# Narrowing MoE2's weights as a pipeline over three pieces, and splitting the token combinations at the MoEs' border from the tiles that form them

## The chip, the cores and the metric

One Trainium2 chip, one of its cores. The metric is the device time of one launch in microseconds (us), lower is better. Three runs of the kernel before gave 1250.58, 1254.18 and 1259.58 us; the median is 1254.18 us.

## The reference, cut to what matters

Attention with talking heads feeds two MoE layers (one expert each) one after the other. Everything is float32 in the reference; the inputs of the MoEs' weights are float64 on the host and reach the chip as 64-bit words.

```python
# attention: batch 4, 12 heads, 448 positions, head_dim 64
scores = softmax(einsum('bhij,hg->bgij', scale * q @ k.T, w_pre))
x = einsum('bhij,hg->bgij', scores, w_post) @ v        # -> [1792 tokens, 768]
# MoE1: w_in 768x1024, w_out 1024x768
h = x @ w_in
solu = h * softmax(h)
x = ((solu - mean) / sqrt(var + 1e-6) * g_ln) @ w_out
# MoE2: w_in 768x2048, w_out 2048x768
g = maximum(x @ w_in, 0) ** 2
out = g @ w_out
```

## The kernel before

The kernel is one program whose order is written by hand: every engine runs its instructions in the order of the code, and a tile's buffers (`bufs=`) decide when an instruction may start. TensorE (PE) multiplies; ScalarE (ACT), VectorE (DVE) and GpSimd (POOL) do the rest; SyncE's queue (SP) issues nearly all DMAs, in order. Float32 products are made of three products of high and low parts, so each operand is split: ACT writes the high part, and DVE or POOL subtracts it to get the low part.

**Stages.** Attention runs to about 406 us. MoE1 follows: a loop over 14 tiles of 128 tokens (m = 0 to 13, line 828). The border between the MoEs finishes MoE1's output products and prepares MoE2 (`prepare`, line 990). MoE2 (line 1170) runs 16 steps q: eight slices of 256 hidden columns for the first half of the tokens, then the same eight for the second half. Its input product is a Strassen-like scheme with seven products p1 to p7 (`prod`) over halves of tokens and of channels, which needs sums and differences of token blocks (`mix_x`) and of weight blocks (`mix_w`).

**A tile of MoE1.** PE does `h1(m)` (36 matmuls), transposes tile m-1 (`zt`, 8) and, from m = 4 on, two output products (`out1`, 24 each). `norm1(m)` takes the negative maximum (DVE, line 712), the exponential (ACT, 715), the gated product and its statistics (DVE, 718 to 723), a power (POOL, 725 and 726), and, behind a yield, the normalisation (ACT, 732). The transposes of the next tile wait for that. In tiles 0 to 3, two blocks of MoE1's output weights are loaded per tile (`load_w1_out`, 683) and split at once by ACT (688) and POOL (689).

**Narrowing.** MoE2's weights arrive as 96 pieces of 128x256 64-bit words. `w2stream` turns each into float32 bits and stores it in HBM, from where MoE2 loads slices. It is a generator: the MoE loops call `steps2(n)` to issue its next n steps between their own instructions. A piece is: ACT squares the high words into `sq` (80), DVE makes the bits in three instructions (83, 87, 91), and values whose square is under 2^-30 are made zero. In MoE1 POOL does that (`flush`, a compare at 100 and a product at 101), in MoE2's first half DVE does (96). `nraw` has three buffers, `nt` two, `nsq` one. 65 pieces are narrowed in MoE1 and 31 in MoE2.

**The border.** `mix_x(0)` loads blocks `xb` of MoE1's output x2D, forms four combinations on DVE and stores them in HBM (`xtD`). `load_xc` then loads each operand again into `xr` (three buffers), and `split_xc` splits it (ACT 925, DVE 926). p1, p6, p5 and p7 are split during the last nine output products, p3, p2 and p4 in the first three slots of step q = 0. For the second half of the tokens POOL does `mix_x` during q = 2 to 6.

Of the kernel before, what the change touches and what calls it, by code (L numbers as in the profile page):

```python
# [18 lines left out]
def kernel(  # L19
# [761 lines left out]
    def w2stream():  # L781

        raws, ready = {}, []

# [12 lines left out]
        load(0)
        load(1)
        for i in range(len(w2pieces)):
            sq = nar_p.tile([128, WP], F32, tag="nsq", name="nsq", bufs=1)  # L800
            t = nar_p.tile([128, WP], F32, tag="nt", name="nt", bufs=2)
            eng = nc.gpsimd if in_first else nc.vector
            for step, _ in enumerate(narrow(raws[i], sq, t, eng)):
                if step == 1:
                    load(i + 2)
                if step == 2 and ready:
                    store()
                yield True
            if eng is nc.gpsimd:
                flush(sq, t)  # L810
# [62 lines left out]
    def mix_x(p, eng):  # L873
# [2 lines left out]
        parts = {}
        for c in range(HC + 1):
            if c < HC:
                qs = []
                for k in range(2):  # L880
                    for t in range(2):
# [383 lines left out]
```

## Time and profile before

| what | value |
|---|---|
| median of three runs | 1254.18 us |
| the profiled execution's own time | 1259.37 us |
| its span, first to last instruction | 1257.6 us |
| mean granted TensorE clock | 0.940 |
| busy share PE, DVE, POOL, ACT | 86%, 59%, 56%, 47% |
| PE busy, 409.7 to 795.7 us | 287.6 of 386.0 us |
| PE busy, 970.7 us to the end | 280.0 of 286.9 us |

A row of the timeline gives the start, the length, the engine, the line and what is written from what; brackets hold the engine's idle time before it and what ended that. A row of a tile's answer gives the shortest, median and longest duration in ns. A row that names an instruction and two numbers below "idle" or "waited" gives microseconds and times.

### The profile page before, as it was taken

The page shows a single profiled execution, that of the slowest core. Times are in us where ns is not written, and L with a number is a line of the kernel's source. Part 1 is how long each engine was busy: PE and PEld are TensorE (multiplying, and loading weights), DVE is VectorE, ACT ScalarE, POOL GpSimd, SP SyncE. Part 2 cuts the span into 40 slices and gives each one's busy share as a digit, 9 for nine tenths or more (in the row PEclk, how much of TensorE's full clock was granted, in tenths as well). Part 3 has the DMA queues.
Part 4 walks back from the last instruction along what each step waited for, and adds up shares of the span by engine and source line. Part 5 has one row for each costly group of instructions (what it writes and reads, how often), then busy time and mean ns, then how long its engine had stood idle before and what let it go on. Part 6 is the DMA issues. An engine that isn't in the chain of part 4 may idle for free.

```text
span 1257.6 us, 31153 instructions
## 1 busy us (share of the span) xinstructions
PE 1083.1 (86%) x12488; PEld 908.4 (72%) x12488; DVE 738.3 (59%) x1293; ACT 585.0 (47%) x1212; POOL 699.9 (56%) x910
## 2 busy tenths in 40 slices
PE   8898979889898855898798666998889999999998
PEld 3555656556667644687687666888778899999998
DVE  3557768658662644555556455778877563344444
ACT  4666666668663322332332224643434556444432
POOL 3657988877755554453554353556654655555531
PEclk9899999989998977898999787999989999999999
DMA  6777887777664433343343485454443352222102
GB/s 178 207 219 221 236 249 219 234 219 209 203 194 121 147 105 112 114 143 97 115 142 107 141 289 163 125 175 142 143 142 106 117 179 99 66 73 63 51 26 88
DMA packets 131936, 187.91 MB, mean 149 GB/s; under 512 B 24752, under 2 KB 104368, under 8 KB 131792
## 3 DMA queue, kind: packets, MB, share of 16 engines
q1 hardware_dynamic: 122948, 161.40, 41.7%
q0 software_dynamic: 6464, 22.60, 6.6%
q10 hardware_dynamic: 2380, 1.93, 0.6%
q8 instruction: 98, 1.61, 0.6%
q14 instruction: 46, 0.38, 0.1%
HBM read 106.45 MB, written 40.89 MB: 117 GB/s over the span
## 4 chain that ended last, share of the span: by engine, by line
PE 20%; DVE 16%; DMA 11%; issue 7%; POOL 6%; ACT 5%; SPq 1%; POOLq 0%; DVEq 0%; ACTq 0%
PE ps_y L1119 11%; PE ps_h L1050 9%; DMA w2iD<-nt 3%; DVE nt L87 2%; POOL nt L101 2%; DMA w2oD<-nt 2%; POOL nsq L100 2%; DMA xr<-x2D 2%; DVE nt L91 2%; DVE y L1130 2%; DMA xr<-xtD 1%; DVE st L721 1%; DVE e L718 1%; DMA w1oraw<-w1oD 1%; DVE nt L83 1%
## 5 line engine op out<-in xcount | busy, mean ns | idle before, releaser
L1119 PE MATMUL ps_y<-to,gt 128*128 128x384 f32 x1332 | 250.9, 342 | 17.5 <-DVE y L1130 17.2
L1119 PEld LDWEIGHTS ps_y<-to,gt 128*128 128x128 f32 x1332 | 238.8, 192 | 24.0 <-DVE y L1130 18.2
L1050 PE MATMUL ps_h<-xc,ti 128*128 128x448 f32 x1008 | 222.4, 373 | 17.1 <-DVE h L1085 10.7
L1050 PEld LDWEIGHTS ps_h<-xc,ti 128*128 128x128 f32 x1008 | 192.0, 192 | 34.9 <-ACT ti L979 11.0
L761 PE MATMUL ps_o<-zt,w1o 128*128 128x384 f32 (+1 forms) x720 | 136.1, 351 | 30.7 <-ACT o L769 27.9
L761 PEld LDWEIGHTS ps_o<-zt,w1o 128*128 128x128 f32 x720 | 130.2, 209 | 35.3 <-ACT o L769 31.7
L299 PEld LDWEIGHTS ps_ring<-w,e 60*64 60x64 f32 (+1 forms) x5760 | 103.3, 138 | 72.1 <-issue 41.1
L318 DVE COPY at<-ps_ring 128x420 f32<-128x420 f32 x156 | 87.8, 610 | 108.5 <-PE ps_ring L299 108.4
L299 PE MATMUL ps_ring<-w,e 60*64 60x60 f32 (+2 forms) x5760 | 112.2, 222 | 31.8 <-issue 23.8
L80 ACT ACTIVATE nsq<-nraw 128x256 f32<-128x256 f32 x96 | 41.7, 434 | 210.0 <-POOL nt L101 145.6
L215 ACT COPY ssrc<-ps_ring 128x896 f32<-128x896 f32 x92 | 82.3, 906 | 107.3 <-PE ps_ring L208 94.0
L459 PE MATMUL ps_h<-w1i,xs 128*128 128x512 f32 x504 | 126.1, 409 | 3.8 <-POOL xs L702 3.4
L1130 DVE TENSOR_TENSOR y<-ps_y,y 128x768 f32<-128x768 f32 x97 | 92.1, 952 | 50.2 <-PE ps_y L1119 50.2
L260 ACT ACTIVATE e<-ps_pre,nm 128x448 f32<-128x448 f32 x180 | 113.1, 639 | 13.7 <-DVE nm L253 10.8
L459 PEld LDWEIGHTS ps_h<-w1i,xs 128*128 128x128 f32 x504 | 97.9, 196 | 27.7 <-POOL xs L702 4.3
L980 POOL TENSOR_TENSOR ti<-s,ti 128x384 fp32r<-128x384 f32 x64 | 69.6, 1099 | 74.1 <-ACT ti L979 72.5
L253 DVE TENSOR_REDUCE nm<-ps_pre 128x1 f32<-128x448 f32 x180 | 103.2, 611 | 12.4 <-PE ps_pre L242 12.4
L208 PE MATMUL ps_ring<-k,q 64*64 64x448 f32 x752 | 100.7, 558 | 5.6 <-ACT ssrc L215 3.7
L242 PE MATMUL ps_pre<-sdst,wpre_bd 64*64 64x448 f32 x720 | 100.5, 570 | 4.4 <-issue 2.7
L1063 DVE TENSOR_TENSOR gt<-h,gt 128x448 fp32r<-128x448 f32 x64 | 48.7, 761 | 92.0 <-ACT gt L1068 90.4
L338 PEld LDWEIGHTS ps_ring<-at,v 128*64 128x64 f32 x1536 | 77.7, 142 | 31.0 <-PE ps_pre L242 12.0
L83 DVE TENSOR_SCALAR nt<-nraw 128x256 uint32<-128x256 uint32 x96 | 39.3, 409 | 94.0 <-DMA w2iD<-nt 53.8
(112 smaller groups left out, 1660.0 us busy)
## 6 DMA issues: line engine op xcount, KB each, us to landing
sdst<-ssrc SPq DMA_DIRECT2D x166, 210.0 KB
nraw<-in_moe_w_in_dram SPq DMA_DIRECT2D x48, 256.0 KB
nraw<-in_moe_w_out_dram SPq DMA_DIRECT2D x48, 256.0 KB
ra<-w2iD SPq DMA_DIRECT2D x32, 384.0 KB
ro<-w2oD SPq DMA_DIRECT2D x32, 384.0 KB
w1raw<-in_moe_w_in_dram POOLq DMA_DIRECT2D x24, 256.0 KB, 6.3
w1raw<-in_moe_w_out_dram POOLq DMA_DIRECT2D x24, 256.0 KB, 5.7
w2iD<-nt SPq DMA_DIRECT2D x48, 128.0 KB
```

The costliest lines, as they stand in the source:

```text
L208: nc.tensor.matmul(out=ps[64 * u:64 * u + 64, e, 0:S], lhsT=qq[c][64 * e:64 * e + 64, p * n + u * half:p * n + u * half + 64], rhs=k[64 * ...
L215: (nc.vector.tensor_copy if dve else nc.scalar.copy)(ssrc[c][:, p:H:HP, :], ps[:, :, 0:S])
L242: nc.tensor.matmul(out=ps[b][64 * u:64 * u + 64, 0:S], lhsT=wpre_bd[64 * r:64 * r + m], rhs=ds[b][64 * r:64 * r + m], start=True, stop=True,)
L253: nc.vector.tensor_reduce(out=nm, in_=pres[s][b][:, 0:S], op=ALU.max, axis=AX.X, negate=True)
L260: nc.scalar.activation(out=e, in_=pres[s][b][:, 0:S], func=AF.Exp, bias=nms.pop((s, b)), scale=1.0, accum_out=sms[s][:, b:b + 1])
L299: nc.tensor.matmul(out=ps[64 * c:64 * c + 64, u, i0:i0 + ng * RH], lhsT=e[64 * u:64 * u + m, o:o + 64], rhs=w[64 * u:64 * u + m, b, g0:g0 ...
L318: nc.vector.tensor_copy(dst[:, 1:3] if u else dst[:, 0:4:3], pv)
L459: nc.tensor.matmul(out=ps[:, u], lhsT=t[:, a, cc], rhs=w1i[cc][:, w, u * 512:(u + 1) * 512], start=(cc == 0 and a == 0 and w == 0), stop=( ...
L761: nc.tensor.matmul(out=ps[:, 0:width], lhsT=w1o[k][:, w, cc * 128:(cc + 1) * 128], rhs=zT[:, a, k, 0:width], start=(k == 0 and i == 0), st ...
L1050: nc.tensor.matmul(out=bank[b][:, 0:HT], lhsT=t[:, w, c], rhs=xc[name][:, a, c], start=(first and c == 0 and i == 0), stop=(c == HC - 1 an ...
L1119: nc.tensor.matmul(out=ps[:, u - u2[0], 0:DM // 2], lhsT=gt[:, a, f, o:o + 128], rhs=w[:, v, f, u * (DM // 2):(u + 1) * (DM // 2)], start= ...
L1130: nc.vector.tensor_tensor(out=yo, in0=po, in1=yo, op=ALU.add)
```

## The change

1. **Narrowing.** The flush goes. In its place ACT squares the high words straight into the result tile, and POOL turns that into a mask of bits in one instruction (compare, times 2 - 2^-23: all bits that the first DVE step may keep, or none). DVE's first instruction ANDs the shifted bits with the mask instead of a constant. The square and the mask of piece i+1 are issued ahead of piece i's DVE work, and the load runs `nr - 1` pieces ahead: five buffers each for `nraw` and `nt` in MoE1, three each in MoE2. A piece is now three steps, with one DVE instruction each.
2. **Its place.** 60 pieces run in MoE1, in groups of 3, 3, 4 and 4 steps per tile (it was 5, 5, 7 and 7 of five-step pieces). 36 run in MoE2, two steps per slot up to slot 9 and one behind it. The second half of `norm1` moves behind the first output product of the tile.
3. **Buffers.** MoE1's loads of x and of output weights use the buffers of the weight preparation; narrowing has no pool of its own any more.
4. **The border.** `prepare` splits p1, p5, p7 and p6 straight from the `xb` tiles as they are formed; only p4's combination goes through HBM.
5. **Second half.** Its combinations are formed with loads further ahead, and its operands are loaded two ahead, every other one into `xb` buffers.

```diff
+    FIRST = 60
-    def w2stream():
+    def w2stream(todo, pool, nr, nt):
...
+        def mask(i):
+            if i in todo:
+                t = ts[i] = pool.tile([128, WP], F32, tag="nt", name="nt", bufs=nt)
+                nc.scalar.activation(out=t, in_=words(i)[1].bitcast(F32), func=AF.Square)
+                nc.gpsimd.tensor_scalar(
+                    out=t, in0=t, scalar1=2.0**-30, scalar2=2.0 - 2.0**-23, op0=ALU.is_ge, op1=ALU.mult
+                )
...
+        for i in range(nr - 1):
+            load(a + i)
+        mask(a)
+        for i in todo:
+            load(i + nr - 1)
+            mask(i + 1)
+            low, high = words(i)
+            bits = ts[i].bitcast(U32)
+            stt = nc.vector.scalar_tensor_tensor
+            stt(out=bits, in0=high, scalar=3, in1=bits, op0=ALU.logical_shift_left, op1=ALU.bitwise_and)
+            yield True
+            if ready:
+                store()
+            stt(out=bits, in0=high, scalar=0xC0000000, in1=bits, op0=ALU.bitwise_and, op1=ALU.bitwise_or)
+            yield True
+            stt(out=bits, in0=low, scalar=29, in1=bits, op0=ALU.logical_shift_right, op1=ALU.bitwise_or)
...
+    stream = w2stream(range(FIRST), m1b_p, 5, 5)
...
-        steps2(5)
+        steps2(3)
         if m > 0:
             zt(m - 1)
-        run(norm)
-        steps2(5)
+        steps2(3)
...
-        for _ in range(2):
+        for i in range(2):
             if outs:
                 out1(*outs.pop(0))
-            steps2(7 if m else 0)
+            steps2(4 if m else 2)
+            if i == 0:
+                run(norm)
+    run(stream)
...
     def prepare():
         load_ra(0)
-        load_xc(0, "p1")
-        mx = mix_x(0, nc.vector)
...
+        parts = [load_xb(0, 0), load_xb(0, 1)]
...
+        for c in range(HC):
+            b11, b12, b21, b22 = qs = parts[c]
+            split_xc(0, "p1", c, b11)
+            yield True
+            mix_x(qs, 0, nc.vector)
+            mix_x(qs, 1, nc.vector)
+            split_xc(0, "p5", c, b11)
+            yield True
+            mix_x(qs, 2, nc.vector)
+            mix_x(qs, 3, nc.vector)
+            split_xc(0, "p7", c, b12)
+            yield True
+            split_xc(0, "p6", c, b22)
+            store_xt(0, c, "p4", b21)
+            if c + 2 < HC:
+                parts.append(load_xb(0, c + 2))
+            split_ti(0, weights.pop(0))
...
     load_xc(0, ORDER[4])
+    load_ra(1)
...
+    in_second = w2stream(range(FIRST, len(w2pieces)), wi2_p, 3, 3)
+    stream = in_second
...
-                steps2(2 if q else 1)
+                steps2(2 if q and k < 10 else 1)
```

What this moves is shown at three places. First, POOL in tile 1 of MoE1: `w1o` are the two blocks of output weights that it splits, `xs` the tokens of tile 3, `nsq`, `nt` the narrowing. Before:

```order
L100 TENSOR_SCALAR nsq<-nsq 128x256
L101 TENSOR_TENSOR nt<-nt,nsq 128x256
L702 TENSOR_TENSOR xs<-xraw,xs 128x768
L689 TENSOR_TENSOR w1o_7718<-w1oraw,w1o_7718 128x768
L689 TENSOR_TENSOR w1o_7721<-w1oraw,w1o_7721 128x768
L100 TENSOR_SCALAR nsq<-nsq 128x256
L101 TENSOR_TENSOR nt<-nt,nsq 128x256
L100 TENSOR_SCALAR nsq<-nsq 128x256
L101 TENSOR_TENSOR nt<-nt,nsq 128x256
```

The same place now, from the end of the tile's statistics on:

```order
L725 TENSOR_TENSOR rs<-rs,eps_sb 128x1
L800 TENSOR_SCALAR nt<-nt 128x256 x2
L701 TENSOR_TENSOR xs<-xraw,xs 128x768
L687 TENSOR_TENSOR w1o_7726<-w1oraw,w1o_7726 128x768
L687 TENSOR_TENSOR w1o_7729<-w1oraw,w1o_7729 128x768
L800 TENSOR_SCALAR nt<-nt 128x256 x2
```

A piece has one POOL instruction in place of two; the masks behind the two splits belong to pieces whose DVE work comes next. Second, DVE at the end of tile 8 of MoE1, up to the maximum of tile 9 (the last row). Before:

```order
L91 SCALAR_TENSOR_TENSOR nt<-nraw,nt 128x256
L83 TENSOR_SCALAR nt<-nraw 128x256
L87 SCALAR_TENSOR_TENSOR nt<-nraw,nt 128x256
L91 SCALAR_TENSOR_TENSOR nt<-nraw,nt 128x256
L83 TENSOR_SCALAR nt<-nraw 128x256
L87 SCALAR_TENSOR_TENSOR nt<-nraw,nt 128x256
L91 SCALAR_TENSOR_TENSOR nt<-nraw,nt 128x256
L83 TENSOR_SCALAR nt<-nraw 128x256
L712 TENSOR_REDUCE nm<-ps_h 128x1
```

Now:

```order
L820 SCALAR_TENSOR_TENSOR nt<-nraw,nt 128x256
L728 SCALAR_TENSOR_TENSOR nb<-mv,rs 128x1
L824 SCALAR_TENSOR_TENSOR nt<-nraw,nt 128x256
L826 SCALAR_TENSOR_TENSOR nt<-nraw,nt 128x256
L820 SCALAR_TENSOR_TENSOR nt<-nraw,nt 128x256
L824 SCALAR_TENSOR_TENSOR nt<-nraw,nt 128x256
L711 TENSOR_REDUCE nm<-ps_h 128x1
```

The bias of the normalisation (`nb`, 728) now stands late in the tile, and L820 needs POOL's mask where L83 needed a free buffer of `nt`. Third, ACT at the start of MoE2's step q = 0: `xc` are the splits of p3, p2 and p4. Before:

```order
L1080 COPY u<-ps_h_10322 128x448
L925 CAST xc<-xr 128x448 x9
L80 ACTIVATE nsq<-nraw 128x256
L979 CAST ti<-ra 128x384
L979 CAST ti<-s 128x384 x2
```

Now:

```order
L1115 COPY u<-ps_h_10113 128x448
L955 CAST xc<-xr 128x448 x3
L799 ACTIVATE nt<-nraw 128x256 x2
L955 CAST xc<-xr 128x448 x6
L799 ACTIVATE nt<-nraw 128x256
```

Two squares of the second narrowing stream, whose loads are issued there, stand ahead of the splits of p2 and p4.

## Rows read from the trace of the kernel before

**Rows 1.** Busy time per stage: stretch, us, then PE, PEld, DVE, ACT, POOL, PEclk, DMA share, GB/s.
```profile
409.70:523.00 113.30, 72.11 (x301) 59.12 (x301) 59.77 (x111) 35.55 (x59) 60.93 (x64) 0.82 0.39 119
523.00:698.60 175.60, 153.53 (x748) 135.78 (x747) 96.16 (x198) 54.30 (x102) 82.26 (x101) 0.95 0.40 123
698.60:762.60 64.00, 41.59 (x256) 40.72 (x255) 33.40 (x50) 19.79 (x42) 24.94 (x24) 0.79 0.63 210
762.60:795.70 33.10, 20.37 (x84) 17.79 (x82) 21.74 (x28) 16.75 (x33) 15.99 (x13) 0.79 0.50 158
795.70:970.70 175.00, 156.17 (x779) 146.28 (x778) 137.29 (x194) 76.39 (x151) 95.47 (x79) 0.95 0.45 143
```

**Rows 2.** Timeline of DVE: maxima of tiles 1, 2, 5, 13; statistics of tile 2.
```profile
418.44 1.21 DVE L712 TENSOR_REDUCE nm<-ps_h 128x1 f32<-128x1024 f32 x1
...
446.06 1.22 DVE L712 TENSOR_REDUCE nm<-ps_h 128x1 f32<-128x1024 f32 x1
...
451.63 0.21 DVE L723 BATCH_NORM_AGGREGATE mv<-st 128x2 f32<-128x12 f32 x1
...
523.04 1.21 DVE L712 TENSOR_REDUCE nm<-ps_h 128x1 f32<-128x1024 f32 x1
...
698.57 1.22 DVE L712 TENSOR_REDUCE nm<-ps_h 128x1 f32<-128x1024 f32 x1
```

**Rows 3.** Timeline of PE in one tile of MoE1 with little waiting.
```profile
637.47 8.59 PE L459 MATMUL ps_h<-w1i,xs 128*128 128x512 f32 x36
647.01 1.09 PE L747 MATMUL ps_tr<-id_sb,e 128*128 128x128 f32 x8 [0.96 <-ACT e L732]
649.30 8.65 PE L761 MATMUL ps_o<-zt,w1o 128*128 128x384 f32 x48 [1.19 <-ACT o L769]
```

**Rows 4.** Tile nt: one instruction's durations, and what ended its engines' idle time.
```profile
L87 DVE SCALAR_TENSOR_TENSOR nt<-nraw,nt x96: 372/426/1973, 415.6 to 965.0; 128x256 uint32<-128x256 uint32 x96
...
  DMA w2iD<-nt: 53.8, 22
...
  DMA w2oD<-nt: 36.4, 13
```

**Rows 5.** Tile nsq: POOL's compare; how long ACT's square waited (us, times).
```profile
L100 POOL TENSOR_SCALAR nsq<-nsq x65: 846/851/1107, 416.6 to 739.1; 128x256 f32<-128x256 f32 x65
...
  ACT nsq L80: 210.0, 73
```

**Rows 6.** Chain that ended last: a load of MoE1's output weights.
```profile
419.11 4.65 DMA w1oraw<-w1oD
```

**Rows 7.** Timeline of POOL: the two splits behind that load.
```profile
423.71 3.66 POOL L689 TENSOR_TENSOR w1o<-w1oraw,w1o 128x768 fp32r<-128x768 f32 x2 [1.48 <-ACT w1o L688]
```

**Rows 8.** Timeline of PE at the border and in q = 0.
```profile
711.42 6.69 PE L761 MATMUL ps_o<-zt,w1o 128*128 128x384 f32 x24 [11.67 <-ACT o L769]
...
751.16 11.59 PE L761 MATMUL ps_o<-zt,w1o 128*128 128x256 f32 x72 [10.62 <-ACT o L769]
...
780.87 7.48 PE L1050 MATMUL ps_h<-xc,ti 128*128 128x448 f32 x27 [10.70 <-DVE h L1085]
```

**Rows 9.** Chain that ended last, border to q = 0: reloads of operands.
```profile
744.85 5.40 DMA xr<-xtD
...
774.91 3.26 DMA xr<-xtD
```

**Rows 10.** DVE's groups from 795.7 to 970.7 us: busy us, mean ns, idle before.
```profile
L1130 DVE TENSOR_TENSOR y<-ps_y,y 128x768 f32<-128x768 f32 x30 | 28.4, 948 | 1.5 <-PE ps_y L1119 1.5
L91 DVE SCALAR_TENSOR_TENSOR nt<-nraw,nt 128x256 uint32<-128x256 uint32 x29 | 25.3, 873 | 0.6
...
L96 DVE SCALAR_TENSOR_TENSOR nt<-nsq,nt 128x256 f32<-128x256 f32 x29 | 22.5, 775 | 1.5
L1063 DVE TENSOR_TENSOR gt<-h,gt 128x448 fp32r<-128x448 f32 x21 | 16.1, 768 | 23.7 <-ACT gt L1068 22.1 <-PE ps_h L1050 1.6
...
L1082 DVE TENSOR_TENSOR u<-ps_h,u 128x448 f32<-128x448 f32 x6 | 3.7, 614 | 0.0
```

More of the change, by code (lines that the diff above doesn't have):

```diff
@@ L681, in load_w1_out @@
     def load_w1_out(kk):
-        r = m1b_p.tile([128, DM], F32, tag="raw", name="w1oraw", bufs=3)
+        r = wi1_p.tile([128, DM], F32, tag="wraw", name="w1oraw", bufs=3)
         nc.sync.dma_start(out=r, in_=w1oD[kk * 128:(kk + 1) * 128, :])
@@ L692, in load_x @@
     def load_x(m):
-        r = m1b_p.tile([128, CC, 128], F32, tag="raw", name="xraw", bufs=3)
+        r = wi1_p.tile([128, CC * 128], F32, tag="wraw", name="xraw", bufs=3)
+        r = r.rearrange("p (c t) -> p c t", c=CC)
         nc.sync.dma_start(
@@ L791, in store @@
         def store():
-            i, t = ready.pop(0)
+            i = ready.pop(0)
             src, dst, k, o = w2pieces[i]
-            nc.sync.dma_start(out=dst[k * 128:(k + 1) * 128, o:o + WP], in_=t)
+            nc.sync.dma_start(out=dst[k * 128:(k + 1) * 128, o:o + WP], in_=ts.pop(i))
             narrowed.append(i)
[L797 to L810, printed above, removed]
+        a = todo[0]
@@ L811, in w2stream @@
             raws.pop(i)
-            ready.append((i, t))
+            ready.append(i)
             yield True
@@ L871, with load_xb @@
     sums = {}
[L873 removed]
+    def load_xb(p, c):
         t0 = 2 * p * HT
[L876 to L881, printed above, removed]
[L882 to L899 removed]
@@ new lines, in load_xb, with mix_x @@
+        qs = []
+        for k in range(2):
+            for t in range(2):
+                b = wi2_p.tile([128, HT], F32, tag=f"xb{k}{t}", name="xb", bufs=2)
+                r0 = (k * HC + c) * 128
+                nc.sync.dma_start(out=b, in_=x2D[r0:r0 + 128, t0 + t * HT:t0 + (t + 1) * HT])
+                qs.append(b)
+        return qs
+    def mix_x(qs, i, eng):
+        b11, b12, b21, b22 = qs
+        out, x, y = ((b11, b12, b11), (b12, b22, b12), (b22, b22, b11), (b21, b21, b22))[i]
+        eng.tensor_tensor(out=out, in0=x, in1=y, op=ALU.subtract)
@@ new lines, with store_xt, mix_second @@
+    XT = ("p5", "p6", "p7", "p4")
+    def store_xt(p, c, name, b):
+        r0 = (XT.index(name) * HC + c) * 128
+        nc.sync.dma_start(out=xtD[p][r0:r0 + 128], in_=b)
+    def mix_second():
+        parts = [load_xb(1, 0), load_xb(1, 1)]
+        yield True
+        for c in range(HC):
+            b11, b12, b21, b22 = qs = parts[c]
+            for i in range(4):
+                mix_x(qs, i, nc.gpsimd)
+                if i % 2:
+                    yield True
+            for name, b in zip(XT, (b11, b22, b12, b21)):
+                store_xt(1, c, name, b)
+            if c + 2 < HC:
+                parts.append(load_xb(1, c + 2))
+            yield True
@@ L906, in load_xc @@
         for c in range(HC):
-            r = wi2_p.tile([128, HT], F32, tag="xr", name="xr", bufs=3)
+            if p and ORDER.index(name) % 2:
+                r = wi2_p.tile([128, HT], F32, tag=f"xb{c // 2}{c % 2}", name="xr", bufs=2)
+            else:
+                r = wi2_p.tile([128, HT], F32, tag="xr", name="xr", bufs=3)
             if name in ("p1", "p2", "p3"):
@@ L1177 @@
             load_xc(*todo[0])
+            load_xc(*todo[1])
         elif q == NE:
```

72 lines of the change are left out of this document (23 added, 49 removed).

## The prediction

> **What bounds the kernel now.** I read the busy time per stage first [rows 1]. From 409.7 to 795.7 us PE is busy for 287.6 of 386.0 us, at a granted clock of 0.82, 0.95, 0.79 and 0.79; behind 970.7 us it is busy for 280.0 of 286.9 us (the table above). So there is time to win in MoE1, at the border and in the first MoE2 steps, and next to nothing later. Attention, ahead of 409.7 us, keeps its order.
>
> Then I looked for the pace of MoE1 in the timeline of DVE: the maxima of tiles 1 and 5 stand at 418.44 and 523.04 us, those of 5 and 13 at 523.04 and 698.57 [rows 2]. That is 26.1 us a tile for four tiles and 21.9 us for eight. PE needs 8.59 + 1.09 + 8.65 = 18.3 us for a full tile [rows 3], and in tiles 1 to 3, without output products, only 9.7. DVE is busy for 96.16 / 8 = 12.0 us a tile behind 523 us, POOL for 10.3, ACT for 6.8 [rows 1]. Nobody is full, so the pace is set by waits. The tile `nt` names them: DVE sat for 53.8 and 36.4 us until a store out of `nt` had landed [rows 4], since it has two buffers; ACT's square waited 210.0 us for the flush, since `nsq` has one [rows 5]. These waits stand in queues that run in order, and what is behind them is the next tile's maximum on DVE and the copies of the output products on ACT.
>
> At the border PE waits 11.67 and 10.62 us for ACT's copies [rows 8]: ACT has casts ahead of them whose operands come back from HBM, 3.26 to 5.40 us per reload [rows 9]. In q = 0 it waits 10.70 us for DVE, which has the splits of p2 and p4 ahead.
>
> **MoE1, tiles 1 to 5.** The flush goes, and the waits for buffers with it. What is late next is the load of output weights. POOL's mask of a piece now stands behind the two `w1o` splits, and DVE needs it ahead of the next maximum (the first order above). In tile 0 nothing stood there before; now the maximum of tile 1 waits for a load of 4.65 [rows 6], ACT's cast, say 0.8, POOL's splits, 3.66 [rows 7], and a mask, 0.85 (the like of L100 [rows 5]): 10 us, so it comes at 428. The tiles that follow repeat one loop: maximum and statistics 5.8 (446.06 to 451.84 [rows 2]); 2.3 pieces of three DVE instructions at 0.43 [rows 4] and the transposes' low parts, put at 1.3, together 4.3; the load, which SP issues behind a load that waits for these pieces, 0.5 + 4.65; cast 0.8, splits 3.66, mask 0.85, one more piece 1.4. That is 22 us against 26.1. Three such tiles bring the maximum of tile 4 to 494. Tile 4 loads no weights; its two output products start with the last split, near 491, and with transposes and `h1(5)` take 18.3: the maximum of tile 5 comes at 509, which is **14 us** earlier.
>
> **MoE1, tiles 5 to 12.** Five buffers and the early mask give a store about four pieces to land. DVE's work stays near 12 us and POOL's falls to some 7, so PE's 18.3 us is next. The bias of the normalisation now stands behind two more pieces, some 3 us; the transposes that need it come a whole `h1` later, so it is covered; uncovered it would cost those 3 us a tile. I take 18.7 us a tile: 8 x (21.9 - 18.7) = **26 us**. Ends: 18.3 (29 us) and 21.9 (nothing). The place of 60 pieces instead of 65 costs MoE1 nothing; the loads in shared `wraw` buffers are issued no later than now.
>
> **The border.** From the maximum of tile 13 to MoE2's first product it is 64.0 us [rows 1]. PE still has six wide output products, 6 x 4.33 [rows 3], six narrow ones at 4.33 x 256 / 384 = 2.9, and two sets of transposes, 2.2: 45.4 us. ACT's copies still stand between casts that wait for DVE's combinations (12 of them and 12 low parts, as now), but nine reloads and nine of twelve stores are gone. I put 5 us of waiting in place of 22: 50 us, a gain of **14 us**. Ends: 46 us, and 64, if DVE's chain of combinations sets the pace.
>
> **q = 0.** ACT has two squares of the new stream ahead of the casts of p2 and p4 (the third order), and their raw words are loaded only there, behind p2's words and 1.5 MB for `ra` and `ro`. So one more load stands in the chain to p5's sum: 3.26 to 5.40 us [rows 9]. I take **5 us more**; ends 0 and 10.
>
> **MoE2, q = 1 to 5.** From 795.7 to 970.7 us DVE adds 30 times to `y` and ACT copies 7, so these are 37 / 7 = 5.3 steps of 33 us. DVE is busy for 137.29 / 5.3 = 25.9 us of a step [rows 1]. 12.8 us of that is not narrowing: 7 x 0.948 + 4 x 0.768 + 5 x 0.614 [rows 10]. L96, 22.5 us in all, goes to POOL, but a step now has 24 narrowing instructions, all of the slow form. At 0.873 (L91) that is 21.0, so 33.8 us a step; with a little waiting 35.5, for four steps: 10 us more. Narrowing then ends in q = 4 and 1.3 steps fall from 33 to PE's 156.17 x 0.95 / 5.3 = 28 us: 6 less. **4 us more**; ends -26 (all steps at 28) and +45 (below). What changes in the second half is hidden behind PE: nothing.
>
> **Sum.** -14 - 26 - 14 + 5 + 4 = -45 us. The profiled execution took 1259.4, so 1214.4; it was 5.2 us above the median of 1254.18, so **1209 us**.
>
> **A rule that speaks against it.** DVE's instructions with two SBUF inputs take longer where POOL works: L91 took 0.873 us on average in the five steps in which POOL was busy for 95 of 175 us, though the like L87 has a median of 0.426; L1082, which reads PSUM, kept 0.614 [rows 1, 4, 10]. The Trainium skill (GPSIMD Engine Reference, 8. Key points) says that POOL shares its SBUF interfaces with VectorE and contends with instructions that read two SBUF inputs. The rows agree with it. By this rule the change exposes one narrowing instruction more per piece and adds a POOL instruction per piece as well, and it leads to the second rival here.
>
> **Rivals.**
> - *Narrowing leaves the path everywhere: 1179 us, chance 0.2.* DVE loses L96 and its waits for stores, falls below PE's pace, and q = 1 to 5 run at 28 us: 5.3 x 5 = 26 us, and the 4 above are not paid. For it: DVE's 25.9 us are under 28. Against it: 24 instructions per step where 22 were.
> - *The shared interface: slower, chance 0.12.* DVE's two-input instructions stretch to x us beside POOL's masks. A tile of MoE1 then needs 5.9 + 14 x on DVE and a step of MoE2 12.8 + 24 x; both pass the forecast near x = 0.93, and behind that each 0.1 costs 8 x 1.4 + 4 x 2.4 = 21 us. No change is reached at x = 1.14 and 1% slower at 1.2; at 1.3 it is 1209 + 77 = 1286 us. For it: the 0.873, and single instructions of 1.973 [rows 4]. Against it: POOL does less in MoE1 than now. I give 0.06 to x from 1.05 to 1.2 and 0.06 to more.
> - *DMA still paces the tiles: 1235 us, chance 0.15.* ACT's squares now write `nt` directly, so they wait for stores as DVE did, and SP stands behind copies of output products. If the tiles stay at 21.9 us, the 26 us are not won.
> - *The border stays: 1223 us, chance 0.06.* DVE's combinations, each followed by a cast, set its pace; the 14 us fall away.
>
> **How the numbers follow.** The forecast has 0.47, with a range of its own of 1192 to 1226 us. A measurement of this kernel tells about 1% (12.5 us) from no change. Below 1241.6 lie the forecast, the first, third and fourth rival: 0.88, of which I leave 0.02 to their upper ends; so 0.86 for faster, 0.08 for no change, 0.06 for slower. The range from 1176 to 1240 leaves out the shared interface's 0.12 and the lower end of the first rival.
>
> **What would show it.** In the trace after: the maximum of tile 1 near 428, of tile 5 near 509, then 18.7 us a tile up to some 660; no idle time of 10 us ahead of output products; first MoE2 product near 710; a wait ahead of p3's product that is longer than 10.7 us; 35 us a step for q = 1 to 4. The prediction is wrong if tiles 5 to 12 stay above 21 us, if DVE's three narrowing instructions average over 1.1 us, or if tiles 1 to 4 run at 18 us or less.

## The result and the profile after

The changed kernel takes 1201.78 us (median of 4 runs, 1198.60 to 1203.72); the kernel before took 1254.57 us beside it on the same chip. The ratio is 0.9575, with a 95% interval of 0.9532 to 0.9617. The forecast was 1209 us, the range 1176 to 1240. The profiled execution took 1203.72 us, with a span of 1201.9.

Busy time per stage of the changed kernel comes first, with the columns of [rows 1]. The stages are MoE1's tiles 0 to 5, its tiles 5 to 13, the border, q = 0, q = 1 to 4, and the rest; a q lasts from the first product into `y` that it issues to the first that the next one issues.

```profile
408.20:508.90 100.70, 63.47 (x262) 53.01 (x261) 61.08 (x114) 34.53 (x61) 55.69 (x46) 0.78 0.45 140
508.90:649.60 140.70, 140.70 (x739) 127.33 (x737) 102.11 (x192) 51.56 (x100) 64.70 (x61) 1.00 0.47 145
649.60:698.10 48.50, 44.55 (x304) 43.78 (x303) 25.93 (x38) 18.03 (x37) 15.42 (x13) 1.00 0.38 129
698.10:737.90 39.80, 20.12 (x83) 17.62 (x83) 23.34 (x30) 16.82 (x34) 22.09 (x18) 0.74 0.48 158
737.90:881.00 143.10, 120.00 (x591) 110.37 (x590) 104.06 (x153) 63.22 (x125) 115.64 (x94) 0.95 0.50 160
881.00:1201.90 320.90, 314.90 (x1684) 301.89 (x1682) 153.78 (x201) 144.06 (x267) 158.76 (x135) 1.00 0.26 87
```

The second row is the one to see: from 508.9 to 649.6 us PE is busy all the time, at a granted clock of 1.00, where [rows 1] had 153.53 of 175.60 us at 0.95. The next two rows show what is left: q = 0 with PE half idle, and q = 1 to 4 with POOL busy for 115.64 of 143.1 us. Stage by stage, in us:

| stage | before | after | difference | forecast |
|---|---|---|---|---|
| attention, to the maximum of tile 0 | 409.7 | 408.2 | -1.5 | 0 |
| tiles 0 to 5 | 113.3 | 100.7 | -12.6 | -14 |
| tiles 5 to 13 | 175.5 | 140.7 | -34.9 | -26 |
| border, to the first MoE2 product | 64.0 | 48.5 | -15.5 | -14 |
| q = 0, to the first product into `y` | 33.1 | 39.8 | +6.7 | +5 |
| q = 1 to 4 | 126.9 | 143.0 | +16.2 | +10 |
| q = 5 to the end | 335.0 | 320.9 | -14.1 | -6 |
| span | 1257.6 | 1201.9 | -55.7 | -45 |

Attention is the same code in every kernel here, and its end scatters between 406.6 and 416.9 us over the runs. So the experiments below are read by stage, and by the time from the maximum of tile 0 to the end ("behind attention"): 847.9 us before, 793.7 after.

The timeline of DVE has the maxima that answer to [rows 2], those of tiles 1, 2, 4, 5 and 13:

```profile
429.66 1.22 DVE L711 TENSOR_REDUCE nm<-ps_h 128x1 f32<-128x1024 f32 x1
450.58 1.22 DVE L711 TENSOR_REDUCE nm<-ps_h 128x1 f32<-128x1024 f32 x1
...
493.13 1.22 DVE L711 TENSOR_REDUCE nm<-ps_h 128x1 f32<-128x1024 f32 x1
508.94 1.22 DVE L711 TENSOR_REDUCE nm<-ps_h 128x1 f32<-128x1024 f32 x1 [1.40 <-PE ps_h L457]
...
649.61 1.22 DVE L711 TENSOR_REDUCE nm<-ps_h 128x1 f32<-128x1024 f32 x1 [2.58 <-PE ps_h L457]
```

The last two wait for PE's product: DVE is early. The first three do not, so in tiles 1 to 4 DVE itself is late. What it waited for stands in the chain that ended last, here from tile 0 to the maximum of tile 1 (start, us, what):

```profile
418.42 5.20 DMA w1oraw<-w1oD
423.65 0.84 ACT w1o L686
424.65 1.67 issue
426.32 1.81 POOL w1o L687
428.22 1.08 POOL nt L800
429.32 0.43 DVE nt L820
429.75 1.14 DVE nm L711
```

It is the chain that the prediction named: the load of an output weight, its cast, its split, the mask, one narrowing instruction, the maximum. (`issue` is time in which the profile shows no wait; POOL split the other block then.)

The timeline of PE answers to [rows 3] (a full tile) and to [rows 8] (the border and q = 0):

```profile
508.74 1.03 PE L746 MATMUL ps_tr<-id_sb,e 128*128 128x128 f32 x8
509.53 8.57 PE L760 MATMUL ps_o<-zt,w1o 128*128 128x384 f32 x48
517.94 8.55 PE L457 MATMUL ps_h<-w1i,xs 128*128 128x512 f32 x36
526.32 1.03 PE L746 MATMUL ps_tr<-id_sb,e 128*128 128x128 f32 x8
...
673.40 7.30 PE L760 MATMUL ps_o<-zt,w1o 128*128 128x384 f32 x48 [1.25 <-ACT o L768]
681.75 6.01 PE L760 MATMUL ps_o<-zt,w1o 128*128 128x256 f32 x48 [1.04 <-ACT o L768]
689.42 8.89 PE L760 MATMUL ps_o<-zt,w1o 128*128 128x256 f32 x72 [1.66 <-ACT o L768]
...
721.86 7.43 PE L1085 MATMUL ps_h<-xc,ti 128*128 128x448 f32 x27 [16.11 <-DVE h L1120]
```

A tile is 526.32 - 508.74 = 17.58 us with no wait in it. The three durations of a tile add up to 18.15, because each record begins some 0.2 us before the one ahead of it ends. At the border the waits of 11.67 and 10.62 us for ACT's copies are down to 1.66 at most; in q = 0 the wait of 10.70 us has grown to 16.11.

In q = 1 to 4 the groups of DVE, ACT and POOL that narrow, and of PE's products into `y`, read so (busy, mean ns, idle before):

```profile
L820 DVE SCALAR_TENSOR_TENSOR nt<-nraw,nt 128x256 uint32<-128x256 uint32 x32 | 25.7, 803 | 21.8 <-POOL nt L800 21.8
L824 DVE SCALAR_TENSOR_TENSOR nt<-nraw,nt 128x256 uint32<-128x256 uint32 x32 | 25.2, 787 | 0.5
...
L826 DVE SCALAR_TENSOR_TENSOR nt<-nraw,nt 128x256 uint32<-128x256 uint32 x32 | 15.8, 495 | 0.6
...
L800 POOL TENSOR_SCALAR nt<-nt 128x256 f32<-128x256 f32 x31 | 35.8, 1156 | 19.7 <-ACT nt L799 17.4
...
L799 ACT ACTIVATE nt<-nraw 128x256 f32<-128x256 f32 x30 | 13.1, 435 | 40.8 <-DMA w2oD<-nt 19.9 <-DMA w2iD<-nt 18.9 <-DVE h L1122 1.8
...
L1154 PE MATMUL ps_y<-to,gt 128*128 128x384 f32 x337 | 69.5, 359 | 17.4 <-DVE y L1165 13.3 <-ACT y L1163 3.0 <-POOL to L1018 1.1
```

Read from the top, this is a chain of waits: DVE for POOL's mask, POOL for ACT's square, the square for a store out of `nt`, and PE for DVE's addition to `y`. The experiments ask which of these is worth time.

### The profile page after: what moved, and what is told of

Same layout as the page of the kernel before. It is cut to its first block, busy times and chain, and to the rows that moved or that the text cites. A ratio compares the mean times of both kernels' runs of the same rounds, so it can differ in the third digit from the quotient of the medians.

```text
span 1201.9 us, 30983 instructions
## 1 busy us (share of the span) xinstructions
PE 1059.8 (88%) x12488; PEld 894.5 (74%) x12488; DVE 722.9 (60%) x1262; ACT 581.3 (48%) x1212; POOL 712.9 (59%) x876
## 3 DMA queue, kind: packets, MB, share of 16 engines
q10 hardware_dynamic: 2380, 1.93, 0.6%
## 4 chain that ended last, share of the span: by engine, by line
PE 63%; DVE 9%; DMA 8%; issue 7%; ACT 6%; POOL 6%; SPq 1%; ACTq 0%; POOLq 0%; DVEq 0%
PE ps_y L1154 14%; PE ps_h L1085 11%; PE ps_o L760 8%; PE ps_h L457 7%; PE ps_ring L297 6%; PE ps_ring L336 6%; PE ps_pre L240 5%; PE ps_ring L206 5%; DMA sdst<-ssrc 3%; POOL nt L800 2%; DVE nt L820 2%; DVE nt L824 1%; ACT ssrc L213 1%; POOL s L994 1%; DVE gt L1098 1%
## 5 line engine op out<-in xcount | busy, mean ns | idle before, releaser
L1085 PEld LDWEIGHTS ps_h<-xc,ti 128*128 128x128 f32 x1008 | 190.4, 190 | 43.2 <-ACT ti L1009 16.5
L800 POOL TENSOR_SCALAR nt<-nt 128x256 f32<-128x256 f32 x96 | 111.8, 1164 | 67.1 <-ACT nt L799 60.5
L297 PE MATMUL ps_ring<-w,e 60*64 60x60 f32 (+2 forms) x5760 | 113.0, 222 | 35.8 <-issue 28.7
L457 PE MATMUL ps_h<-w1i,xs 128*128 128x512 f32 x504 | 126.9, 412 | 0.0
L760 PE MATMUL ps_o<-zt,w1o 128*128 128x384 f32 (+1 forms) x720 | 122.0, 328 | 4.0 <-ACT o L768 4.0
L760 PEld LDWEIGHTS ps_o<-zt,w1o 128*128 128x128 f32 x720 | 118.2, 190 | 4.7 <-ACT o L768 4.7
L258 ACT ACTIVATE e<-ps_pre,nm 128x448 f32<-128x448 f32 x180 | 113.3, 640 | 15.4 <-DVE nm L251 12.4
L1098 DVE TENSOR_TENSOR gt<-h,gt 128x448 fp32r<-128x448 f32 x64 | 53.9, 842 | 94.6 <-ACT gt L1103 94.4
L820 DVE SCALAR_TENSOR_TENSOR nt<-nraw,nt 128x256 uint32<-128x256 uint32 x96 | 55.3, 576 | 66.7 <-POOL nt L800 66.7
```

Of the source, the lines that this page charges most:

```text
L258: nc.scalar.activation(out=e, in_=pres[s][b][:, 0:S], func=AF.Exp, bias=nms.pop((s, b)), scale=1.0, accum_out=sms[s][:, b:b + 1])
L297: nc.tensor.matmul(out=ps[64 * c:64 * c + 64, u, i0:i0 + ng * RH], lhsT=e[64 * u:64 * u + m, o:o + 64], rhs=w[64 * u:64 * u + m, b, g0:g0 ...
L457: nc.tensor.matmul(out=ps[:, u], lhsT=t[:, a, cc], rhs=w1i[cc][:, w, u * 512:(u + 1) * 512], start=(cc == 0 and a == 0 and w == 0), stop=( ...
L760: nc.tensor.matmul(out=ps[:, 0:width], lhsT=w1o[k][:, w, cc * 128:(cc + 1) * 128], rhs=zT[:, a, k, 0:width], start=(k == 0 and i == 0), st ...
L800: nc.gpsimd.tensor_scalar(out=t, in0=t, scalar1=2.0**-30, scalar2=2.0 - 2.0**-23, op0=ALU.is_ge, op1=ALU.mult)
L1085: nc.tensor.matmul(out=bank[b][:, 0:HT], lhsT=t[:, w, c], rhs=xc[name][:, a, c], start=(first and c == 0 and i == 0), stop=(c == HC - 1 an ...
```

## The experiments

All but the first are edits of the changed kernel that keep the rest of it. The ratio stands to the kernel before on the same chip. By their intervals only the early output weights, fewer steps and the last two lie clear below the changed kernel; the others overlap with it and are read by stage, from one profiled execution each. Stages that a run does not touch scatter: tiles 0 to 5 from 99.8 to 101.9 us, q = 0 from 39.6 to 41.3, q = 1 to 4 from 143.0 to 145.0. A difference inside such a range shows nothing.

| run | ratio (95% interval) | behind attention | what moved against the changed kernel |
|---|---|---|---|
| changed kernel | 0.9575 (0.9532 to 0.9617) | 793.7 | |
| three buffers | 0.9584 (0.9548 to 0.9620) | 796.0 | tiles 5 to 13: +1.6, else within the scatter |
| early output weights | 0.9492 (0.9454 to 0.9529) | 785.9 | tiles 0 to 5: -8.3 |
| flush, square ahead | 0.9509 (0.9459 to 0.9558) | 787.5 | tiles 0 to 5: -7.6 |
| border as before | 0.9621 (0.9573 to 0.9669) | 801.5 | border: +9.2 |
| primed stream | 0.9543 (0.9495 to 0.9592) | 792.3 | q = 0: -1.7, border +1.1, q = 1 +2.7, q = 2 -3.1 |
| late start in q = 0 | 0.9526 (0.9474 to 0.9578) | 793.9 | q = 0: -0.9, q = 1 -0.9, q = 5 +0.8 |
| fewer steps per q | 0.9489 (0.9459 to 0.9519) | 787.4 | q = 1 to 4: -12.8, q = 5 +5.7 |
| no mask in MoE2 | 0.9499 (0.9440 to 0.9559) | 785.2 | q = 1 to 4: -6.6 |
| store early | 0.9558 (0.9508 to 0.9609) | 792.5 | q = 1 to 4: -2.6 |
| combinations late | 0.9596 (0.9537 to 0.9655) | 795.1 | q = 1 to 4: -3.4, later +4 |
| three together | 0.9466 (0.9418 to 0.9513) | 777.2 | tiles 0 to 5 -5.3, tiles 5 to 13 +3.8, border +2.9, q = 1 to 4 -21.1, q = 5 +3.1 |
| three, late start | 0.9401 (0.9344 to 0.9458) | 773.4 | tiles 0 to 5 -6.9, tiles 5 to 13 +2.5, border +3.5, q = 0 -2.3, q = 1 to 4 -21.6, q = 5 +4.9 |

### MoE1: are the buffers the reason?

```diff
-    stream = w2stream(range(FIRST), m1b_p, 5, 5)
+    stream = w2stream(range(FIRST), m1b_p, 3, 3)
```

> The changed kernel with three buffers each for the raw words and the results in MoE1 (it has five), all else as changed. Theory, the buffers let the stores land: ACT's square of piece i+1 now waits for a store issued one piece earlier, so tiles 5 to 12 rise from 17.6 to 19.5 us or more and the time to 1217 or more. Rival, what freed the tiles is that POOL's flush went: they stay at 17.6 us and the time near 1202.

With three buffers tiles 5 to 12 take (652.18 - 509.93) / 8 = 17.78 us each, against 17.58 with five, though ACT's square now waits 38.8 and 38.5 us there for stores out of `nt`. The prediction gave the five buffers as the reason that stores land in time; that falls.

### MoE1: is the load of output weights late in tiles 1 to 4?

```diff
+        for kk in range(len(w1o), min(K1, len(w1o) + 2)):
+            wr[kk] = load_w1_out(kk)
         if m:
             run(h1(m))
...
-        for kk in range(len(w1o), min(K1, len(w1o) + 2)):
-            wr[kk] = load_w1_out(kk)
```

> The changed kernel with the loads of MoE1's output weights issued at the start of a tile instead of behind six narrowing steps. Theory, the load of about 5 us stands in the loop of tiles 0 to 3: their maxima come every 17 us instead of 21, tile 5's at 491 to 494 instead of 509, and the time is about 1185. Rival, POOL's and DVE's own work paces these tiles: less than 5 us come of it, the time is 1197 or more.

Tiles 0 to 5 fall from 100.7 to 92.4 us: the load is on the path, but for 8.3 us, where 15 to 18 were expected. What stays is seen in the timeline of this run's DVE and POOL:

```profile
456.62 2.06 POOL L701 TENSOR_TENSOR xs<-xraw,xs 128x768 fp32r<-128x768 f32 x1
...
457.04 1.93 DVE L824 SCALAR_TENSOR_TENSOR nt<-nraw,nt 128x256 uint32<-128x256 uint32 x1
...
458.65 3.92 POOL L687 TENSOR_TENSOR w1o<-w1oraw,w1o 128x768 fp32r<-128x768 f32 x2
459.00 1.91 DVE L826 SCALAR_TENSOR_TENSOR nt<-nraw,nt 128x256 uint32<-128x256 uint32 x1
...
462.65 2.46 POOL L800 TENSOR_SCALAR nt<-nt 128x256 f32<-128x256 f32 x2
463.75 0.42 DVE L820 SCALAR_TENSOR_TENSOR nt<-nraw,nt 128x256 uint32<-128x256 uint32 x1 [2.84 <-POOL nt L800]
```

A narrowing instruction that takes 0.42 us elsewhere takes 1.93 and 1.91 beside POOL's splits of 2.06 and 1.98 us (the second is the first of the two in 3.92), and ends 0.28 us behind each; then DVE waits 2.84 us for a mask that had these splits ahead of it.

### MoE1: was it the flush that went, or the square that came earlier?

```diff
+                if i < FIRST:
+                    sqs[i] = pool.tile([128, WP], F32, tag="nsq", name="nsq", bufs=3)
+                    nc.scalar.activation(out=sqs[i], in_=words(i)[1].bitcast(F32), func=AF.Square)
+                    return
...
+            if i < FIRST:
+                nc.vector.tensor_scalar(
+                    out=bits, in0=high, scalar1=3, scalar2=0x3FFFFFFF, op0=ALU.logical_shift_left, op1=ALU.bitwise_and
+                )
+            else:
...
+            if i < FIRST:
+                flush(sqs.pop(i), ts[i])
...
-    stream = w2stream(range(FIRST), m1b_p, 5, 5)
+    stream = w2stream(range(FIRST), m1b_p, 3, 3)
```

In MoE1 this brings back the flush of the kernel before, with its two POOL instructions behind the piece, but issues the square one piece ahead, into one of three `nsq`.

> The run with three buffers each, with the flush of the kernel before in MoE1 in place of the mask: POOL compares and multiplies behind DVE's third instruction, with three buffers for the squares, which are still issued a piece ahead. Theory, what freed the tiles is that no buffer is waited for and the square runs ahead: tiles 5 to 12 stay at 17.6 to 18.3 us. Rival, the flush itself at the end of a piece's chain held them: 19.5 us or more, and the time rises by 12 us or more.

Tiles 5 to 12 take (641.37 - 500.98) / 8 = 17.55 us, as with the mask, though POOL is busy for 83.92 us there in place of 64.70. So the flush was not by itself what held these tiles. The kernel before had it with one `nsq` and two `nt`, and no square ahead; with look-ahead either form leaves the path.

Where PE waited before is in its groups from 523.0 to 698.6 us:

```profile
L761 PE MATMUL ps_o<-zt,w1o 128*128 128x384 f32 x396 | 77.1, 354 | 5.6 <-ACT o L769 5.6
...
L747 PE MATMUL ps_tr<-id_sb,e 128*128 128x128 f32 x64 | 10.7, 321 | 16.5 <-ACT e L732 16.5
```

Of 22.1 us of idle time 16.5 stood ahead of the transposes, which waited for ACT's normalisation; that in turn waited 15.4 us for its bias from DVE. The change also moved this normalisation, the second half of `norm1`, and every run here keeps the move. So at least three things are not separated by any run: the square ahead, a third `nt`, and the new place of the normalisation.

In tiles 0 to 5 the flush is even the better form, 93.1 against 100.7 us. The timeline of DVE at tile 1, of the changed kernel first and then of this run:

```profile
429.32 0.43 DVE L820 SCALAR_TENSOR_TENSOR nt<-nraw,nt 128x256 uint32<-128x256 uint32 x1 [7.68 <-POOL nt L800]
429.66 1.22 DVE L711 TENSOR_REDUCE nm<-ps_h 128x1 f32<-128x1024 f32 x1
```

```profile
418.69 1.64 DVE L825 TENSOR_SCALAR nt<-nraw 128x256 uint32<-128x256 uint32 x1 [0.17 <-DMA w2iD<-nt]
420.25 1.21 DVE L711 TENSOR_REDUCE nm<-ps_h 128x1 f32<-128x1024 f32 x1
```

A mask has to be there before DVE's first instruction on the piece, and so before all that is queued behind it, the maximum too; the flush comes after DVE's last one, and only the store waits for it.

### The border

```diff
-        parts = [load_xb(0, 0), load_xb(0, 1)]
+        load_xc(0, "p1")
+        mx = mix_old(0, nc.vector)
...
```

`mix_old` stands for the border of the kernel before: combinations stored, and loaded again for their splits.

> The changed kernel with the border of the kernel before: combinations formed, stored to HBM and loaded again before they are split, the weights of the second slice loaded within it. Theory, the reloads hold ACT and with it PE: from tile 13's maximum to MoE2's first product it takes 58 us or more in place of 48.5, q = 0 takes 34 to 36 in place of 39.8, since nothing but p2's and p4's words is loaded there, and the time is 1206 to 1212. Rival, the border was long only because DVE and ACT came to it a tile late: it stays within 3 us of 48.5, and with a shorter q = 0 the time is 1199 or less.

The border takes 709.83 - 652.16 = 57.7 us in place of 48.5, and a wait like the ones of [rows 8] is back, by the timeline of PE:

```profile
698.82 11.18 PE L760 MATMUL ps_o<-zt,w1o 128*128 128x256 f32 x72 [10.88 <-ACT o L768]
```

That is 0.3 short of the 58 or more that were expected. So 9.2 of the 15.5 us come from the border's own edit. The other 6.3 are there with the old border too; the granted clock over it was 0.88 here, 0.79 before and 1.00 after, but no run separates the clock's part. q = 0 is no shorter (39.6 us, where 34 to 36 were expected), so its loss does not come from this edit.

### q = 0: does the second stream's start cost the 6.7 us?

The first run issues the stream's first step in the border; the second issues no steps in slots 0 to 2 of q = 0.

```diff
+    for n, (g, cc) in enumerate(outs):
...
+        if n == 6:
+            steps2(1)
```

> The changed kernel with the first step of the second narrowing stream (its first loads, squares, masks) issued ahead of the seventh of the border's last nine output products. Theory, the raw words' load stands in q = 0 in the chain to p5's sum: q = 0 falls from 39.8 to 34 us and the time to 1196. Rival, the 1.5 MB for the next slices' weights ahead of p2's and p4's words set that wait: q = 0 stays within 1.5 us of 39.8.

```diff
-                steps2(2 if q and k < 10 else 1)
+                steps2(0 if q == 0 and k < 3 else 2 if q and k < 10 else 1)
```

> Edit: no narrowing steps of the second stream in slots 0 to 2 of q=0; the 24 steps a q are otherwise as in the changed kernel and end that much later. Theory: the steps stand ahead of the gated multiplies of the first products on VectorE; then the wait ahead of the product of position 3 falls from 16.1 us to about the 10.7 of the kernel before, q=0 from 39.8 to about 34 us, and the time to about 1196 us. Rival: the second stream only starts later, and the wait comes back further on in q=0 or in q=1, as it did when the stream was started in the border; then the first y product stands earlier but q=1 is longer by as much, and the time stays within 3 us of 1202.

Both shorten the wait ahead of p3's product, from 16.11 to 11.97 and 13.35 us; in runs that leave q = 0 alone it is 15.73 us or more. Little comes of it: primed, q = 0 is 38.1 us, the border 49.6, q = 1 36.6 in place of 33.9 and q = 2 31.4 in place of 34.5, in all 1.4 us less; with the late start q = 0 is 38.9 us, just below the scatter, and the time behind attention 793.9, as before. So the stream does stand in the way of the first products, but moving it by itself gains next to nothing. The chain that ended last in the changed kernel shows how it stands there:

```profile
706.57 5.89 DMA nraw<-in_moe_w_in_dram
712.48 0.43 ACT nt L799
712.90 1.40 ACT xc L955 x3
714.35 2.49 DVE xc L956 x3
716.86 2.54 DMA xr<-xtD
```

ACT's square waits for raw words ahead of the casts of p2 and p4, and the load of p4's operand comes only behind these; p4's split stands ahead of p5's sum on DVE, and p3's product waits for that sum.

### q = 1 to 4: the number of steps, the mask, the stores, the combinations

Fewer steps a q, 17 in place of 24, so that the stream lasts longer:

```diff
-                steps2(2 if q and k < 10 else 1)
+                steps2(2 if q and k in (3, 6, 9) else 1)
```

> The changed kernel with 17 narrowing steps per step q in place of 24, so that narrowing ends in q = 6 instead of q = 4. Theory, DVE's load per step sets the pace of q = 1 to 4: they fall from 35.8 to about 30 us, q = 5 and 6 rise by 1 to 2, and the time is about 1180. Rival, a piece costs its microsecond wherever it stands: q = 1 to 4 fall, q = 5 and 6 take it back, and the time stays at 1198 to 1204.

q = 1 to 4 take 130.2 us (expected 120) and q = 5 33.2 in place of 27.5: 12.8 us won and 5.7 given back. Behind attention the kernel is 6.3 us shorter, where about 22 were expected. q = 1, without combinations of the second half, takes 28.9 us; q = 2 to 4 take 31.3, 35.3 and 34.7.

Without POOL's masks in MoE2, so that the part of the narrowing which the mask does is left out there:

```diff
-                nc.gpsimd.tensor_scalar(...)
+                if i < FIRST:
+                    nc.gpsimd.tensor_scalar(...)
```

> The changed kernel without POOL's mask instruction in MoE2's first half (36 pieces); small weights there are then not set to zero and bits are lost, all else is computed. Theory, POOL's masks slow DVE, by the shared SBUF interfaces and by the wait for the mask: DVE's three narrowing instructions fall from a mean of 0.69 to 0.55 us, its 21.8 us of waiting for the mask go, q = 1 to 4 fall from 143 to about 125 us, the time to 1185. Rival, PE waits there for something else: q = 1 to 4 stay at 138 or more.

q = 1 to 4 fall by 6.6 us, to 136.5. DVE's groups in this run:

```profile
L821 DVE SCALAR_TENSOR_TENSOR nt<-nraw,nt 128x256 uint32<-128x256 uint32 x31 | 27.7, 892 | 7.9 <-ACT nt L799 7.9
L825 DVE SCALAR_TENSOR_TENSOR nt<-nraw,nt 128x256 uint32<-128x256 uint32 x32 | 23.9, 746 | 0.5
L827 DVE SCALAR_TENSOR_TENSOR nt<-nraw,nt 128x256 uint32<-128x256 uint32 x32 | 21.5, 672 | 0.6
```

The wait of 21.8 us for masks is gone (7.9 us for ACT's square are there now), but the instructions take 73.1 us together in place of 66.7, though POOL now does 79.0 us of work there and not 115.64. So taking the masks away did not make DVE's instructions shorter. What the masks cost is the wait for them, and 6.6 us of it in the balance; the outcome lies between the 125 us of the theory and the 138 or more of its rival.

The store of a piece issued right behind its last instruction:

```diff
-            if ready:
-                store()
...
             ready.append(i)
+            store()
```

> The changed kernel with each piece's store issued right behind its third DVE instruction, a step earlier. Theory, in MoE2, with three result buffers, ACT's square waits for that store (38.8 us of its idle time in q = 1 to 4) and what is behind it in ACT's queue holds PE: the wait falls below 20 us, q = 1 to 4 from 143 to 136 or less, the time to 1195. Rival, ACT's wait is off the path: the wait falls, q = 1 to 4 stay at 141 or more.

q = 1 to 4 are 140.5 us, 2.6 less. ACT's wait only changes its name, by ACT's groups:

```profile
L799 ACT ACTIVATE nt<-nraw 128x256 f32<-128x256 f32 x31 | 13.5, 436 | 42.1 <-DMA nraw<-in_moe_w_out_dram 22.5 <-DMA nraw<-in_moe_w_in_dram 17.8 <-DVE nt L824 1.2
```

The combinations of the second half, moved from q = 2 to 5 into q = 5 and 6:

```diff
-                if 2 <= q < NE - 1 and k in (2, 6, 10):
+                if 5 <= q < NE - 1 and k in (1, 3, 5, 7, 9, 11):
```

> Edit: the combinations of the second half of the tokens (mix_second) are issued in q=5 and q=6 alone, in place of from q=2 on; all else as in the changed kernel. Theory: in q=2 to 4 GpSimd's combinations and its narrowing share stand in one queue, and the masks behind them hold VectorE and so TensorE. Then q=2 to 4, which take 36.6 us each in the changed kernel, fall to about 33, q=5 and 6 rise by 2 us each at most, and the time is about 1194 us. Rival: VectorE's own queue of narrowing and multiplies sets these steps, so that q=2 to 4 stay at 35.5 us or above and the time stays within 3 us of 1202.

q = 2 to 4 take 33.2, 36.3 and 36.0 us, 35.2 on average against 36.4, and q = 5 to the end pays 4 us for it; behind attention it is 795.1 us. POOL's busy time in q = 1 to 4 falls from 115.64 to 101.44 us and PE still waits 12.2 us for DVE. POOL's combinations are not what sets these steps.

No single wait there was worth more than 7 us; the number of narrowing steps was. On average over q = 1 to 4 a q takes 35.8 us with 24 steps, 32.6 with 17, and in the last two runs 30.5 and 30.4 with 14; without any it takes 27.5. The averages hide a spread. With 14 steps q = 1, 2 and 4 take 27.5 to 29.2 us, but q = 3 takes 36.7 and 37.3. Its row in the last run:

```profile
792.85:830.20 37.35, 31.18 (x149) 29.00 (x147) 26.95 (x33) 13.51 (x27) 30.43 (x25) 0.91 0.46 145
```

PE waits 2.93 us there for POOL's split of output weights and 3.24 us for ACT, which had sat 6.74 us until a store out of `nt` had landed; and at a granted clock of 0.91 PE's own work takes 31.18 us in place of 27.8 in q = 2. The changed kernel shows the clock's part too: 0.91 in q = 3 and 4, with PE busy for 31.27 and 31.42 us, against 1.00 in q = 1 and 2 with 28.67 and 28.58. So some 5.4 us of its 143 are TensorE's slower clock, beside 23.1 us of idle time. No run separates these causes.

### Three together

The third part, which was not run by itself, takes twelve pieces from MoE2 into MoE1's tiles, where DVE is busy for only 102.11 / 8 = 12.8 of 17.58 us; the others are the early weights and the flush with the square ahead.

```diff
-    FIRST = 60
+    FIRST = 72
...
-            steps2(4 if m else 2)
+            steps2(5 if m else 2)
...
-                steps2(2 if q and k < 10 else 1)
+                steps2(1)
```

> Edit: three together. The loads of the next output weight are issued at the start of a tile; the narrowing of MoE1 keeps the flush in place of the mask, with the square issued one piece ahead and three buffers of each kind; and the second stream takes 72 steps in MoE1's tiles (three or five a tile) and one step a slot in MoE2. Theory: the gains stand in different stages and add: tiles 0 to 5 in about 88 us (100.7 in the changed kernel), the later tiles at 17.6 us each as TensorE sets them, q=1 to 4 at 29 to 30 us each (35.8), in all about 1165 us. Rival: the steps that are moved into MoE1's tiles take room that VectorE and the transfers have not got there; the tiles rise above 18.5 us each, or q=1 to 4 stay above 33 us, and the time is 1185 us or more.

The last run differs from this one by a line:

```diff
-                steps2(1)
+                steps2(1 if q or k > 2 else 0)
```

> Edit: as the run before (early output weights, flush with the square ahead, 72 steps in MoE1), and no narrowing steps in slots 0 to 2 of q=0. Theory: with the steps away from the first products q=0 is shorter by 4 to 6 us, and nothing gives it back, as the second stream is far ahead; so 4 to 6 us less than the run before. Rival: the wait ahead of the product of position 3 has another cause, its inputs' loads; then the same time within 2 us.

Together they take 777.2 us behind attention, 16.5 less than the changed kernel, where 37 were expected. q = 1 to 4 do what was expected, 121.9 us. Tiles 5 to 12 rise to 18.05 us, 4 more in all; the border takes 51.4 us, and q = 5, where narrowing now ends, 30.6. Tiles 0 to 5 are 95.4 us, above either part alone: early weights and the flush take away the same wait, so their gains don't add, and two more steps a tile cost some of it. With the late start q = 0 is 37.5 us in place of 40.2, and q = 5 gives back 1.8. Its 773.4 us behind attention are 3.8 less than the run before, but only 1.4 of that stands behind the first MoE2 product; the rest stands in MoE1 and the border, where the two have the same code, and is scatter. So of the 8 us between the medians (1193.58 and 1185.58) the late start is not shown to give more than some 1.4. Its stages:

```profile
410.40:504.20 93.80, 63.24 (x270) 52.76 (x269) 77.85 (x122) 36.48 (x63) 67.36 (x70) 0.82 0.51 152
504.20:647.40 143.20, 140.91 (x732) 126.33 (x732) 118.28 (x210) 55.68 (x106) 92.43 (x111) 1.00 0.53 160
647.40:699.40 52.00, 45.97 (x305) 45.05 (x304) 31.91 (x51) 19.42 (x41) 23.27 (x23) 0.97 0.48 155
699.40:736.80 37.40, 21.56 (x82) 18.86 (x82) 20.11 (x28) 18.80 (x37) 20.08 (x16) 0.73 0.48 154
736.80:858.30 121.50, 114.66 (x590) 108.17 (x590) 85.04 (x111) 55.87 (x110) 95.10 (x80) 0.97 0.47 149
```

This kernel is the fastest of the study, 1185.58 us at a ratio of 0.9401 (0.9344 to 0.9458). PE is now idle for 30.6 us in tiles 0 to 5 and 15.8 in q = 0, and for 6.8 in q = 1 to 4.

## Why the prediction was right

The forecast is 7 us above the median. By its own steps, in the profiled executions (1214.4 forecast, 1203.7 taken):

- **Tiles 1 to 5, -14: -12.6.** The loop was forecast at 22 us and took 20.92, 20.92 and 21.63; maxima forecast at 428, 494 and 509 stand at 429.66, 493.13 and 508.94. The early weights show that the load was in the path, the flush run that the mask's wait behind the splits was. The first was worth 8.3 of the 15 to 18 us that it was later expected to give.
- **Tiles 5 to 12, -26: -34.9.** This is the term that was mis-sized. PE does set the pace, as forecast, but at 17.58 and not at 18.7 us. The prediction added three durations of one tile [rows 3] to 18.3 and put 0.4 of waiting on top. The records overlap, so the step from one start to the next is shorter than the sum, and there was no waiting. 8 x 1.1 = 9 us, which is most of the 10.7 us between forecast and run. DVE's share was right (12.8 us a tile, 12 forecast); POOL's mask takes 1.13 us (the median), not 0.85. Of the 34.9 us, 22.1 were idle time; the other 12.8 came off PE's busy time, as the granted clock went from 0.95 to 1.00 (the stretch before also holds 396 output matmuls, the one after 384).
- The reason given for this pace, five buffers, was wrong: three do as well, and so does the flush. Both runs keep what the prediction hardly spoke of, the square one piece ahead, a third `nt`, and the new place of the normalisation; which of these frees the tiles stays open. The prediction also put the waits before at DVE's maximum and ACT's copies, while PE lost 16.5 us at transposes behind the normalisation and 5.6 at copies. And of the 210.0 us in [rows 5] 145.6 were for the flush; 64.4 were for DVE's line 96 in MoE2.
- **Border, -14: -15.5.** Right in size; its own edit holds 9.2 us of it.
- **q = 0, +5: +6.7.** The sign and place were right; one load more stands in the chain. But moving the stream's start alone gave back 1 to 2 us there, and 1.4 us or nothing in the total: the wait that grew is there, and the two squares are only a part of it.
- **MoE2, +4: +2.1.** This small miss is in part luck: +16.2 stands for +10 and -14.1 for -6, and the two nearly cancel. A step was forecast at 35.5 and takes 35.8 us, from the wrong parts: the narrowing instructions average 66.7 / 96 = 0.69 us, not 0.873, and waits take the difference, that for masks among them. Of the other term only the balance can be compared: the forecast spread the time before evenly, at 33 us a step, while four steps there took 31.7 and one, from 922.57 us on, 40.2.
- **Rivals.** *Narrowing leaves the path everywhere* did not come true: in MoE1's full tiles it left the path, as forecast, but q = 1 to 4 take 35.8 us a step and not 28. *DMA still paces the tiles* and *the border stays* are refuted by the rows above. *The shared interface* does not decide: mean durations stay under the 0.93 us from which it would have. It is there in single instructions, as the early-weights run shows beside POOL's splits. The Trainium skill (GPSIMD Engine Reference, 8. Key points) says that POOL shares SBUF interfaces with VectorE and contends with instructions that read two SBUF inputs; those rows agree with it, 1.93 us in place of 0.42, while in the run without masks fewer POOL instructions did not make DVE's shorter.

## What to carry to other kernels

Put a step on another engine where only the end waits for it: a pass that must come before the first instruction on a queue that runs in order holds all that is behind it, and a pass at the end holds only the store. Take the pace of an engine from the distance of two like starts in an unbroken stretch, not from the sum of durations. Ask for each added instruction which stage has that engine idle: twelve pieces moved to such a stage took 21 us off q = 1 to 4 and cost about 10 elsewhere, by the stages of a run with two other edits; no single wait that was taken away gave as much as that balance.
